# Reordered first loads, merged score matmuls and a split last tile in a fused recurrence and gated-MLP kernel

## Chip, cores, metric

One core of one Trainium2 chip. The metric is the device time of one execution in microseconds (us), as a median over executions; lower is better. The medians quoted are over all runs. A ratio is the mean time of one kernel's fast runs over that of the kernel before in the same rounds on the same chip, so it isn't quite the ratio of the medians that are quoted.

## The reference, cut

```python
# q, k, v, f_logit: (batch 4, heads 8, seq 768, dim 48), float32
f = 1 / (1 + exp(-f_logit))
for t in range(S):
    state = f[:, :, t, :, None] * state + einsum('bhd,bhe->bhde', k[:, :, t], v[:, :, t])
    y[:, :, t] = einsum('bhd,bhde->bhe', q[:, :, t], state)
x = y as (3072 tokens, 384)
out = (relu(x @ w_gate) * (x @ w_val)) @ w_out        # 384 -> 1536 -> 384
```

The kernel cuts the sequence into 6 steps of 128 tokens; a step has 4 chunks, one for each batch. Loads come for two batches at a time ("first pair" and "second pair", written 01 and 23 below). A chunk needs a cumulative sum of log f on TensorE (from f), exponentials on ScalarE, the scaled q and k (called hats), their transpose (qkT), scores, a mask, y, and a state update. The MLP of the step before runs on TensorE in between.

## The kernel before

It is a list scheduler that runs when the kernel is built. Each operation is declared with what it reads and writes and with a planned duration: `occ`, how long it holds its engine, and `lat`, what follows until others may use its result. The scheduler simulates the engines and picks the operation that can start first. The outcome is one fixed order of instructions for each engine. The planned durations are in no instruction; they only decide the order. On the chip each engine goes through its list and waits where an input isn't there yet.

```python
class Plan:
    def schedule(self, banks):
        ...
            for e in self.ENGINES:
                for op in waiting[e]:
                    at = max(free[e], op.ready)
                    ...                                  # a free PSUM bank, if it opens one
                    key = (at, op.prio, op.idx)
                    if pick is None or key < pick[0]:
                        pick = (key, op, slot)
        ...
            op.start, op.end = at, at + op.occ + op.lat
            free[e] = at + op.occ
# --- cut ---
early = ("f0.0.1 f0.1.2 f0.2.3 f0.3.4 k0.0.1 k0.1.2 q0.0.1 q0.1.2 v0.0.1 ...").split()
spread_engines = ['ACT', 'DVE', 'ACT', 'ACT']
pl = Plan({"bc": 1, "tp": 1, "s": 2, "y": 1, "kv": 1, "f": 4, "w": 1})     # banks by kind
pl.settled, pl.margin = 40.0, {"PE": 0.5, "SP": 0.6}
# --- cut: loads are issued by SyncE; so are qkT and x transposes (steps 3 to 5) and stores ---
def cum():
    te.matmul(bc.ap[:, 0:HD], tri[:, :], bn[:, :, 0:D])
    for p in range(NP):
        mm = te.matmul(bc.ap[:, HD + p:HD + p + 1], ..., ones[:, :])
    return mm
chain("cum", "PE", cum, [...], [bc], occ=0.48, lat=PE_L, prio=P, opens=[bc])
# --- cut ---
sA, sB = Bank("s"), Bank("s")
chain("scores", "PE", scores, qk_key, [sA, sB], occ=0.36, lat=PE_L, prio=P + 5, opens=[sA, sB])
```

## Time and profile before

| | before |
|---|---|
| median (range), first 3 runs | 201.19 us (200.59 to 201.33) |
| profiled span | 198.9 us |
| TensorE busy, idle in the span | 192.1 us, 6.8 us |
| TensorE idle in 0-40, 40-105, 105-155 us | 1.62, 0.04, 2.25 us |

The last row comes from the view of busy time by stretch: the width of the stretch minus TensorE's busy time. Its columns are the stretch, its width, then busy us (and instructions) of PE, PEld, DVE, ACT and POOL, the granted clock, the share of busy transfer engines, and GB/s.

```profile
0.00:40.00 40.00, 38.38 (x441) 30.98 (x442) 25.14 (x63) 27.94 (x65) 19.34 (x39) 1.00 1.13 198
40.00:105.00 65.00, 64.96 (x743) 45.48 (x740) 43.82 (x89) 44.06 (x116) 41.62 (x53) 1.00 1.10 209
105.00:155.00 50.00, 47.75 (x398) 25.21 (x399) 26.10 (x41) 28.06 (x57) 16.23 (x20) 1.00 0.81 164
```

The chain of work that ended last (start, us, what) passes through a last transfer at 108.63 and is TensorE alone from 116.13 on:

```profile
99.32 4.14 DMA f_in<-in_f_logit_dram
...
108.63 4.98 DMA q_in<-in_q_dram
...
115.63 0.46 POOL vpad L556
116.13 0.34 PE ps L716 x4
116.48 1.29 PE ps L748 x6
```

SyncE's timeline around the last loads (start, duration with the wait in it, what):

```profile
123.62 1.94 SPq L397 DMA_DIRECT2D f_in<-in_f_logit_dram  x1
125.60 2.73 SPq L785 DMA_DIRECT2D out_dram<-osb  x1
128.78 0.37 SPq L397 DMA_DIRECT2D k_in<-in_k_dram  x1
129.21 2.50 SPq L622 DMA_TRANSPOSE qkT<-hats  x1
```

### The profile page before, as it was taken

To read this page: it belongs to the slowest core of one execution; us is meant where nothing else is said; L and a number is where in the kernel's file an instruction comes from. 1 tells how busy PE (TensorE), PEld (TensorE's weight loads), DVE (VectorE), ACT (ScalarE), POOL (GpSimd) and SP (SyncE) were. 2 spreads that over 40 slices of the span, in tenths; PEclk is the share of its full clock that TensorE was granted. 3 is DMA by queue.
4 is the path that set the end of the run, shared out by engine and by line. 5 is a ranking of instruction groups with operands and counts; after the bars stand their busy time and mean duration, and the time that the engine had idled before them with its cause. 6 is when DMAs were issued, how large, how long until landed. Compare 5 with 4: busy or idle time off the path is not lost.

```text
span 198.9 us, 4530 instructions
## 1 busy us (share of the span) xinstructions
PE 192.1 (97%) x1796; PEld 122.9 (62%) x1796; DVE 107.0 (54%) x208; ACT 115.1 (58%) x263; POOL 77.2 (39%) x111
## 2 busy tenths in 40 slices
PE   7999999999999999999997989999999999999994
PEld 5887588866888787745553535555545555544552
DVE  7258865574399787647737443636265233443300
ACT  2786767906888677867649466386425433344311
POOL 5189303733859668693573174504500000000000
PEclk9999999999999999999999999999999999999999
DMA  4999999999979999999798899988942200111112
GB/s 118 232 225 198 201 214 187 209 222 243 254 173 227 193 240 177 198 212 207 158 213 167 174 185 202 215 171 187 190 112 59 63 31 9 40 40 43 40 71 87
DMA packets 118180, 31.74 MB, mean 160 GB/s; under 512 B 111248, under 2 KB 118160, under 8 KB 118160
## 3 DMA queue, kind: packets, MB, share of 16 engines
q1 hardware_dynamic: 114176, 27.93, 70.3%
q0 software_dynamic: 3984, 3.54, 11.2%
q8 instruction: 14, 0.23, 0.5%
q14 instruction: 6, 0.05, 0.1%
HBM read 25.95 MB, written 4.72 MB: 154 GB/s over the span
## 4 chain that ended last, share of the span: by engine, by line
PE 78%; DMA 10%; SPq 5%; ACT 3%; POOL 2%; issue 1%
PE ps L748 43%; PE ps L770 22%; SPq L397 4%; DMA wv<-in_moe_w_val_dram 4%; PE ps L636 3%; DMA q_in<-in_q_dram 3%; DMA f_in<-in_f_logit_dram 2%; DMA k_in<-in_k_dram 2%; PE ps L613 2%; PE ps L675 2%; PE ps L716 2%; PE ps L671 2%; PE ps L580 1%; ACT relu L755 1%; POOL hats L603 1%; PE ps L582 1%
## 5 line engine op out<-in xcount | busy, mean ns | idle before, releaser
L759 DVE TENSOR_TENSOR gT<-relu,ps 128x256 bf16<-128x256 bf16 (+1 forms) x96 | 52.1, 551 | 59.1 <-PE ps L748 41.4
L748 PE MATMUL ps<-xT,wv 128*128 128x256 bf16 (+1 forms) x288 | 62.5, 326 | 0.5 <-DMA wv<-in_moe_w_val_dram 0.5
L748 PE MATMUL ps<-xT,wg 128*128 128x256 bf16 (+1 forms) x288 | 62.5, 326 | 0.1
L755 ACT ACTIVATE relu<-ps 128x256 bf16<-128x256 f32 (+1 forms) x96 | 46.0, 490 | 27.6 <-PE ps L748 27.3
L770 PE MATMUL ps<-wo,gT 128*128 128x384 bf16 x288 | 52.2, 326 | 0.0
L770 PEld LDWEIGHTS ps<-wo,gT 128*128 128x128 bf16 x288 | 26.6, 97 | 16.8
L748 PEld LDWEIGHTS ps<-xT,wv 128*128 128x128 bf16 x288 | 26.1, 97 | 16.6 <-DMA wv<-in_moe_w_val_dram 0.6
L642 DVE TENSOR_TENSOR ptm<-ps,tri 128x512 bf16<-128x512 f32 x48 | 31.0, 684 | 9.8 <-PE ps L636 9.6
L748 PEld LDWEIGHTS ps<-xT,wg 128*128 128x128 bf16 x288 | 26.6, 98 | 15.2 <-DMA xT<-xn 0.8
L782 ACT ACTIVATE osb<-ps 128x384 f32<-128x384 f32 x24 | 11.7, 491 | 31.7 <-PE ps L770 31.7
L600 POOL TENSOR_TENSOR hats<-k_in,expo 128x384 bf16<-128x384 f32 x20 | 19.9, 997 | 17.6 <-ACT expo L589 17.6
L603 POOL TENSOR_TENSOR hats<-q_in,expo 128x384 bf16<-128x384 f32 x20 | 19.8, 998 | 11.2 <-DMA q_in<-in_q_dram 11.2
L732 POOL TENSOR_TENSOR st<-ssum,dec 128x384 bf16<-128x384 f32 x16 | 13.2, 829 | 14.6 <-DVE ssum L730 14.6
L453 PE MATMUL ps<-zeros 128*128 128x256 bf16 x96 | 14.3, 307 | 1.1 <-DVE zeros L357 1.1
L689 ACT ACTIVATE xn<-ps 128x384 bf16<-128x384 f32 x20 | 9.8, 490 | 6.0 <-PE ps L675 6.0
L556 POOL CAST vpad<-v_in 128x384 bf16<-128x384 f32 x24 | 12.1, 518 | 2.3 <-DMA v_in<-in_v_dram 2.2
L589 ACT ACTIVATE expo<-ps 128x384 f32<-128x384 f32 x20 | 9.8, 491 | 4.0 <-PE ps L582 3.8
L453 PEld LDWEIGHTS ps<-zeros 128*128 128x128 bf16 x96 | 10.1, 110 | 3.2 <-DVE zeros L357 1.1
L570 ACT ACTIVATE f_in<-f_in 128x768 f32<-128x768 f32 x10 | 8.4, 838 | 4.4 <-DMA f_in<-in_f_logit_dram 4.4
L730 DVE TENSOR_TENSOR ssum<-ps,st 128x384 f32<-128x384 f32 x16 | 8.8, 551 | 2.7 <-PE ps L716 2.6
L636 PE MATMUL ps<-qkT 48*128 48x128 bf16 x192 | 9.5, 219 | 0.6 <-DMA qkT<-hats 0.6
L591 ACT ACTIVATE expo<-ps 128x384 f32<-128x384 f32 x20 | 9.9, 495 | 0.0
(71 smaller groups left out, 153.5 us busy)
## 6 DMA issues: line engine op xcount, KB each, us to landing
out_dram<-osb SPq DMA_DIRECT2D x24, 192.0 KB, 2.2
f_in<-in_f_logit_dram SPq DMA_DIRECT2D x10, 384.0 KB, 5.8
k_in<-in_k_dram SPq DMA_DIRECT2D x10, 384.0 KB, 5.2
q_in<-in_q_dram SPq DMA_DIRECT2D x10, 384.0 KB, 5.4
v_in<-in_v_dram SPq DMA_DIRECT2D x10, 384.0 KB, 5.4
wg<-in_moe_w_gate_dram POOLq DMA_DIRECT2D x3, 384.0 KB, 7.2
wv<-in_moe_w_val_dram POOLq DMA_DIRECT2D x3, 384.0 KB, 7.4
wo<-in_moe_w_out_dram POOLq DMA_DIRECT2D x3, 384.0 KB, 7.3
```

The lines of the kernel that those rows point to most:

```text
L453: op = add("PE", lambda: te.matmul(cold.ap[:, 0:256], zeros[:, 0:128], zeros[:, :]), ["zeros"], [cold], occ=0.22 if i < 17 else 0.11, lat= ...
L556: add("POOL", lambda: gp.tensor_copy(vout, vin[:, b, :, :].rearrange("p (n j) d -> p n j d", j=2)), [f"v{li}_{b}", f"vpad{vi}"], [f"v_{vi} ...
L600: add("POOL", lambda: gp.tensor_tensor(hk, kin[:, b, :, :], ex[:, 1, :].rearrange("p (h d) -> p h d", h=H), ALU.mult), [f"k{li}_{b}", f"ex ...
L603: add("POOL", lambda: gp.tensor_tensor(hq, qin[:, b, :, :], ex[:, 0, :].rearrange("p (h d) -> p h d", h=H), ALU.mult), [f"q{li}_{b}", f"ex ...
L636: mm = te.matmul(s.ap[:, p * C:(p + 1) * C], qkT[qi][lo:lo + D, 1, p, :], qkT[qi][lo:lo + D, 0, p, :])
L642: add("DVE", lambda j=j, s=s: ve.tensor_tensor(ptm[mi][:, j, :, :], s.ap[:, :].rearrange("p (n t) -> p n t", n=NP), mask, ALU.mult), [s, " ...
L732: add("POOL", lambda: gp.tensor_tensor(t4(s_new), t4(tmp), rate, ALU.mult), [key] + dk, [f"S{b}_{c % 2}"], prio=P + 8, **pool_t(HD))
L748: mm = te.matmul(bank.ap[:, 0:n], wt[:, kt, j * 128:(j + 1) * 128], xT[xi][:, kt, n0:n1], start=(kt == 0), stop=(kt == NK - 1))
L755: add("ACT", lambda: sc.activation(relu[ri][:, 0:n], gate.ap[:, 0:n], AF.Relu), [gate], [f"relu{ri}"], prio=P, **act_t(n))
L759: add("DVE", lambda: ve.tensor_tensor(gT[gi][:, j, n0:n1], relu[ri][:, 0:n], val.ap[:, 0:n], ALU.mult), [val, f"relu{ri}"], [f"gT{gi}_{j}_ ...
L770: mm = te.matmul(o.ap[:, 0:DM], gT[gi][:, j, b * C:(b + 1) * C], wo[:, j, :], start=(j == 0), stop=(j == NJ - 1))
L782: add("ACT", lambda o=o, oi=oi: sc.activation(osb[oi][:, :], o.ap[:, 0:DM], AF.Copy), [o], [f"osb{oi}"], prio=P, **act_t(DM))
```

## The change

Its intent: k and q of the first pair are loaded ahead of the second pair's f, so that the first scores come earlier; the first spread copies (transposed q and k out of PSUM) start on VectorE; the scores of two chunks stand in one run in steps 4 and 5, so that TensorE goes over to their 48-row form half as often; the last 128 rows of the output are computed as 256 and 128 columns, so that the last copy and store are short. With them three planned durations change: cumulative sum 0.48 to 0.29, scores 0.36 to 0.42 for one chunk and 0.64 for two, and the latency of the zeroing in front of the first matmuls 0.2 to 0.9.

```diff
-    early = ("f0.0.1 f0.1.2 f0.2.3 f0.3.4 k0.0.1 k0.1.2 q0.0.1 q0.1.2 v0.0.1 v0.1.2 ...
+    early = ("f0.0.1 f0.1.2 k0.0.1 k0.1.2 q0.0.1 q0.1.2 f0.2.3 f0.3.4 v0.0.1 v0.1.2 ...
-    spread_engines = ['ACT', 'DVE', 'ACT', 'ACT']
+    spread_engines = ['DVE', 'ACT', 'DVE', 'ACT']
+    TAIL = [0, 256, 384]
+    PAIR = [1, 1, 1, 1, 2, 2]
-    pl = Plan({..., "s": 2, ...})
+    pl = Plan({..., "s": 4, ...})
-    zero("DVE", ve, zeros[:], "zeros", 128, -20)
+    zero("DVE", ve, zeros[:], "zeros", 128, -20, 0.9)          # planned latency
-            chain("cum", "PE", cum, [...], [bc], occ=0.48, ...)
+            chain("cum", "PE", cum, [...], [bc], occ=0.29, ...)
-        chain("scores", "PE", scores, qk_key, [sA, sB], occ=0.36, ...)
+        yield P, qk_key, scores, [sA, sB]
+    def attend(c, bs):
+        works = [attention(c, b) for b in bs]
+        heads = [next(x) for x in works]
+        def scores():
+            for h in heads:
+                mm = h[2]()
+            return mm
+        chain("scores", "PE", scores, [x for h in heads for x in h[1]], sbanks,
+              occ=0.2 + 0.22 * len(heads), ...)
# --- cut: the output projection of the last chunk loops over the column parts of TAIL,
#     each with its own bank, copy and store ---
-        for b in range(B):
-            attention(c, b)
+        n = PAIR[c]
+        for b in range(0, B, n):
+            attend(c, range(b, b + n))
```

More of the change, by code (lines that the diff above doesn't have):

```diff
@@ L240, in bass_hgrn2_outer__then__ffn_reglu_kernel @@
     wsteps = 3
-    early = ("f0.0.1 f0.1.2 f0.2.3 f0.3.4 k0.0.1 k0.1.2 q0.0.1 q0.1.2 v0.0.1 v0.1.2 k0.2.3 k0.3.4 "
+    early = ("f0.0.1 f0.1.2 k0.0.1 k0.1.2 q0.0.1 q0.1.2 f0.2.3 f0.3.4 v0.0.1 v0.1.2 k0.2.3 k0.3.4 "
              "q0.2.3 q0.3.4 v0.2.3 v0.3.4 wg0 wv0 wg1 wv1 wg2 wv2 f1.0.2 k1.0.2 q1.0.2 v1.0.2 wo0 wo1 "
@@ L315, in bass_hgrn2_outer__then__ffn_reglu_kernel @@
     banks = [nc.alloc_psum_tensor(f"ps{i}", [128, 512], F32) for i in range(8)]
-    pl = Plan({"bc": 1, "tp": 1, "s": 2, "y": 1, "kv": 1, "f": 4, "w": 1})
+    pl = Plan({"bc": 1, "tp": 1, "s": 4, "y": 1, "kv": 1, "f": 4, "w": 1})
     pl.settled, pl.margin = 40.0, {"PE": 0.5, "SP": 0.6}
@@ L354, in bass_hgrn2_outer__then__ffn_reglu_kernel, with zero @@
     add("POOL", lambda: gp.memset(ones[:], 1.0), [], ["ones"], occ=0.1, prio=-8)
-    def zero(eng, e, t, name, cols, prio):
-        add(eng, lambda: e.memzero(t), [], [name], occ=0.15 + cols / 2000.0, prio=prio)
-    zero("DVE", ve, zeros[:], "zeros", 128, -20)
+    def zero(eng, e, t, name, cols, prio, lat=0.2):
+        add(eng, lambda: e.memzero(t), [], [name], occ=0.15 + cols / 2000.0, lat=lat, prio=prio)
+    zero("DVE", ve, zeros[:], "zeros", 128, -20, 0.9)
     for i in range(NB):
@@ L584, in cum @@
                 return mm
-            chain("cum", "PE", cum, ["tri", "ones", f"bneg{bi}", f"bn{bi}_{bj}"], [bc], occ=0.48, lat=PE_L,
+            chain("cum", "PE", cum, ["tri", "ones", f"bneg{bi}", f"bn{bi}_{bj}"], [bc], occ=0.29, lat=PE_L,
                 prio=P, opens=[bc])
@@ L638, in scores @@
             return mm
-        chain("scores", "PE", scores, qk_key, [sA, sB], occ=0.36, lat=PE_L, prio=P + 5, opens=[sA, sB])
+        yield P, qk_key, scores, [sA, sB]
         mask = tri[:].unsqueeze(1).to_broadcast([128, NP, C])
@@ L733, in attention @@
                     [key] + dk, [f"S{b}_{c % 2}"], prio=P + 8, **pool_t(HD))
+    def attend(c, bs):
[5 more added lines that the diff above has]
+            return mm
+        sbanks = [x for h in heads for x in h[3]]
+        chain("scores", "PE", scores, [x for h in heads for x in h[1]], sbanks, occ=0.2 + 0.22 * len(heads), lat=PE_L,
+              prio=heads[0][0] + 5, opens=sbanks)
+        for x in works:
+            for _ in x:
+                pass
     def ffn_hidden(c, b0, b1, j):
@@ L764, in ffn_out, with proj_out @@
         gi = g % NG
-        outs = [Bank("f") for b in bs]
-        def proj_out(o, b, s):
+        cuts = TAIL if (g, bs[-1]) == (NC - 1, B - 1) else [0, DM]
+        parts = [(b, n0, n1, Bank("f")) for b in bs for n0, n1 in zip(cuts, cuts[1:])]
+        def proj_out(o, b, s, n0, n1):
             def run():
                 for j in range(s * OJ, (s + 1) * OJ):
-                    mm = te.matmul(o.ap[:, 0:DM], gT[gi][:, j, b * C:(b + 1) * C], wo[:, j, :],
+                    mm = te.matmul(o.ap[:, 0:n1 - n0], gT[gi][:, j, b * C:(b + 1) * C], wo[:, j, n0:n1],
                                    start=(j == 0), stop=(j == NJ - 1))
@@ L773, in proj_out, with rows @@
             return run
-        for s in range(NJ // OJ):
+        def rows(b, n0, n1, o, s):
             js = range(s * OJ, (s + 1) * OJ)
-            for o, b in zip(outs, bs):
-                P = (g + 1) * B * 10 + 5 + NJ * 3 + b * 3
-                chain("ffn", "PE", proj_out(o, b, s), [f"gT{gi}_{j}_{b}" for j in js] + sorted({f"wo{j // WJ}" for j in js}),
-                      [o], occ=pe_t(*[DM] * OJ), lat=PE_L, prio=P + 1000, opens=[o] if s == 0 else [])
-        for o, b in zip(outs, bs):
+            P = (g + 1) * B * 10 + 5 + NJ * 3 + b * 3
+            chain("ffn", "PE", proj_out(o, b, s, n0, n1), [f"gT{gi}_{j}_{b}" for j in js] + sorted({f"wo{j // WJ}" for j in js}),
+                  [o], occ=pe_t(*[n1 - n0] * OJ), lat=PE_L, prio=P + 1000, opens=[o] if s == 0 else [])
+        if len(cuts) > 2:
+            for part in parts:
+                for s in range(NJ // OJ):
+                    rows(*part, s)
+        else:
+            for s in range(NJ // OJ):
+                for part in parts:
+                    rows(*part, s)
+        for b, n0, n1, o in parts:
             oi, P = (g * B + b) % NO, (g + 1) * B * 10 + 5 + NJ * 3 + b * 3
-            add("ACT", lambda o=o, oi=oi: sc.activation(osb[oi][:, :], o.ap[:, 0:DM], AF.Copy), [o], [f"osb{oi}"],
-                prio=P, **act_t(DM))
-            dst = bass.AP(tensor=out.tensor, offset=(b * S + g * C) * DM, ap=[[DM, C], [1, DM]])
-            op = add("SP", lambda dst=dst, oi=oi: sy.dma_start(dst, osb[oi][:, :]), [f"osb{oi}"], [f"out{g}_{b}"],
+            add("ACT", lambda o=o, oi=oi, n0=n0, n1=n1: sc.activation(osb[oi][:, n0:n1], o.ap[:, 0:n1 - n0], AF.Copy), [o], [f"osb{oi}_{x}" for x in TAIL[:-1] if n0 <= x < n1],
+                prio=P, **act_t(n1 - n0))
+            dst = bass.AP(tensor=out.tensor, offset=(b * S + g * C) * DM + n0, ap=[[DM, C], [1, n1 - n0]])
+            op = add("SP", lambda dst=dst, oi=oi, n0=n0, n1=n1: sy.dma_start(dst, osb[oi][:, n0:n1]), [f"osb{oi}_{x}" for x in TAIL[:-1] if n0 <= x < n1], [f"out{g}_{b}_{n0}"],
                      occ=0.2, lat=0.9, prio=P)
-            dma(op, f"osb{oi}", 0.45)
+            dma(op, f"osb{oi}_{n0}", 0.45 * (n1 - n0) / DM)
     OJ = 4
```

## The prediction

> **What bounds the kernel now.** I read the page first (busy shares, the 40 slices), then the chain of work that ended last in order of time, then the waits of TensorE by stretch, then the timeline around the places that the change touches. The page:
>
> ```profile
> PE 192.1 (97%) x1796; PEld 122.9 (62%) x1796; DVE 107.0 (54%) x208; ACT 115.1 (58%) x263; POOL 77.2 (39%) x111
> PE   7999999999999999999997989999999999999994
> DMA  4999999999979999999798899988942200111112
> ```
>
> TensorE is busy nearly throughout, and the transfer engines are full for the first 24 slices (to about 119 us), after which they are nearly idle. TensorE's busy time at the start isn't work, though: 96 of its matmuls multiply zeros (14.3 us). So there are four stretches: a start in which real work waits for data (to about 22 us), a long stretch without a gap on TensorE (22 to 105), a stretch with gaps while the loads are still running (105 to 117), and pure TensorE work (117 to 196) with a tail of one copy and one store. The chain shows the start:
>
> ```profile
> 10.02 4.04 DMA k_in<-in_k_dram
> 14.15 0.95 POOL hats L506
> 15.10 7.03 DMA wv<-in_moe_w_val_dram
> 22.18 0.50 PE ps L748 x3
> 22.68 0.33 PE ps L636 x8
> ```
>
> The hidden layer's second weight (wv, first third) is issued by GpSimd at 15.10, behind a GpSimd product that waits for the second pair's k, and lands at 22.1. From 22.18 the chain is TensorE alone. The first weight (wg) is issued on the same queue at 12.84, behind a cast that waits for v, and took 7.2 us, so it landed at 20.04, while xT of the first pair was ready at 20.03:
>
> ```profile
> 10.70 1.81 DVE L506 TENSOR_TENSOR hats<-q_in,expo 128x384 bf16<-128x384 f32 x2 [4.34 <-DMA q_in<-in_q_dram]
> 12.38 0.51 POOL L556 CAST vpad<-v_in 128x384 bf16<-128x384 f32 x1 [0.29 <-DMA v_in<-in_v_dram]
> 12.84 0.93 POOL L417 DMA_DIRECT2D wg<-in_moe_w_gate_dram  x1
> 20.18 0.24 PEld L748 LDWEIGHTS ps<-xT,wg 128*128 128x128 bf16 x3
> ```
>
> The waits of TensorE between 100 and 118 us, the only real ones after the start (2.18 us unrounded):
>
> ```profile
> PE ps L716 <- POOL vpad L556: 0.9, 1, 0.9
> PE ps L580 <- ACT bneg L573: 0.6, 1, 0.6
> PE ps L636 <- DMA qkT<-hats: 0.6, 1, 0.6
> ```
>
> Behind each stands a transfer: f of step 4 (second pair, issued at 99.32), the transpose of hats, and q and v of step 4 (issued only at 108.63 and 109.26). Last, the timeline around one group of scores, and the tail:
>
> ```profile
> 86.11 0.81 PE L748 MATMUL ps<-xT,wg 128*128 128x512 bf16 x3
> 86.85 0.23 PEld L636 LDWEIGHTS ps<-qkT 48*128 48x128 bf16 x8 [0.42 <-issue]
> 87.18 0.82 PE L748 MATMUL ps<-xT,wv 128*128 128x512 bf16 x3
> ...
> 188.06 7.96 PE L770 MATMUL ps<-wo,gT 128*128 128x384 bf16 x48
> ...
> 196.06 0.49 ACT L782 ACTIVATE osb<-ps 128x384 f32<-128x384 f32 x1 [1.46 <-PE ps L770]
> ```
>
> **What the Trainium skill says.** "TensorEngine Tiling (Array Packing)", Tiling Modes, Key Properties: changing the tiling mode drains TensorE. Scores use 48 of 128 rows, and the trace agrees in kind: 11 times the weight loads of the scores sat idle with nothing to wait for, 3.9 us in total, though most of that lies under matmuls. "TensorE: Matmul & The Clock Gate", Back-to-back issue gap: a matmul of N columns takes N/2.4 + 2.5 ns, but a stream of weight loads with 128-column matmuls about 81 ns each. For 384 columns the trace agrees with the formula (48 matmuls in 7.81 us, 163 ns); for 128 columns the transposes here take 0.45 us for 8, 56 ns, so I use 56 and keep 81 as a risk. "DMA: Bandwidth & Descriptors", Anatomy of one DMA: about 2 us of a transfer are fixed, and only the rest grows with its bytes. The stores here (192 KB) land in 2.2 us (median), which agrees.
>
> **Part 1, the start.** Two loads of f (second pair) move behind k and q of the first pair. An issue takes 0.65 to 0.68 us of the SP queue, so k and q of the first pair start 1.35 us earlier. The second q load was issued at 5.65 and landed at about 10.6; it should land at about 9.2. Also the first cumulative sum came at 8.20 only because 43 zero matmuls stood before it (its input was ready at 6.92); now 37 stand there, and it starts at about 7.5. With copies of 0.67 us on DVE and ACT I get first scores at about 13.4 instead of 15.10 and xT of the first pair at about 17.7 instead of 20.03.
>
> But this gain meets the weights. v of the first pair is issued in the same slot (6.33), so the cast at 12.38 and wg at 12.84 stay; k of the second pair keeps its slot (8.50), so the product at 14.15 and wv at 15.10 stay. wg lands at 20.0, wv at 22.1, as before. What is left of the gain is what TensorE does while it waits for wv: the fourth batch's scores and back transpose are done before 22.1, not after. Between 22.18 and 25.22 the old kernel ran 4 groups of the hidden layer, one scores, two states and two intra products; the new one lacks the scores (0.33) and has fewer changes of mode (some 0.2): TensorE gains about 0.5 us by 25 us. Of this only about 0.3 survives the first cumulative sum of step 1: it stands behind as many hidden matmuls as before (111), ran at 35.64, and its input from ACT was ready at 34.50 + 0.84 = 35.34, tied to a load that is gated by the weights' landing. **Start: 0.3 us.**
>
> **Part 2, scores of two chunks in a run.** The three hidden matmuls at 86.11 need 0.65 us, so scores could start at 86.76; they start at 86.85: 0.09 us for going over. With 8 groups in steps 4 and 5 becoming 4, four such changes go, 4 x 0.09 = **0.36 us**. Nothing is added in instructions; masks and hats are the same. The four banks that two scores hold take DVE four masks of some 0.6 us, 2.6 us in a row, against one hidden pair each 1.3 us; a short TensorE wait for a bank is possible there.
>
> **Part 3, the order of transfers (a consequence).** The built order shows that on the SP queue q of step 4's second pair now goes out before the four transposes of x and hats, right after k (at about 101 instead of 108.63), while its v stays behind them (about 109). On TensorE one hidden group of 0.65 us moves ahead of the cumulative sum that waited 0.64; hidden work of step 3 now starts before step 4's scores. Worked through: that wait shrinks to about 0.3; x of step 3 lands at about 108.3 (the old kernel began that work at 109.74, but with 0.75 us of scores already done); five hidden groups (3.24), 12 output matmuls (1.95) and scores (0.75) lead to 114.25, where the state product waits for v, 109.3 + 5.4 landing + 0.5 cast = 115.3, against 116.13. So TensorE is ahead by about 0.75 us there, which contains the 0.3 of the start: **0.45 us** of its own. After that I find no wait: step 5's loads come earlier than before.
>
> **Part 4, the last rows.** 12 matmuls of 384 columns become 12 of 256 (109 ns) and 12 of 128 (56 ns): 1.31 + 0.67 = 1.98 against 1.95. The last copy has 128 columns: 512 columns take ACT 0.60 and 384 take 0.49, so 0.11 per 128, estimate 0.27, a gain of 0.22. The last store is 64 KB instead of 192 and shares nothing with the first part, which leaves 0.5 us earlier: of the 2.35 us from the copy's end to the span's end I take 0.25 off. **Tail: 0.45 us**, nothing else beside it.
>
> **Sum:** 0.3 + 0.36 + 0.45 + 0.45 = 1.56 us, so 201.19 - 1.6 = **199.6 us**.
>
> **The rivals.** (a) The start's gain arrives whole: xT 2.3 us earlier. For it: nothing on TensorE, DVE or ACT stands against it. Against it: both weights and step 1's load are tied to GpSimd's order and to full transfer engines, and neither moves. It would make 198 us. (b) The loads alone set the time up to 117 us: the same bytes come through engines that are full to then, so parts 1 and 3 give nothing and only 2 and 4 remain, 200.4 us. For it: the DMA row. Against it: one wait in the old kernel came from q waiting behind transposes, not from bytes. (c) A new wait: scores of two chunks need both transposes landed and four free banks, and a static order can't step round a late one; each such wait was 0.4 to 0.9 us in the old kernel. With two of them the gain is gone, 201 us. (d) The last matmuls run at 81 ns: 0.3 us less gain.
>
> **Range and chances.** Runs of the old kernel lie within 0.4%, so the spread is mine, not the clock's. (b) and (c) give 200.4 to 201, (a) 198; I take 198.5 to 200.8. Over 2% means 4.0 us: more than all four parts together with (a). Faster 0.05, within 2% 0.93, slower 0.02.
>
> **What would show it right or wrong.** Right: first scores near 13.4, first hidden matmuls still near 20.1 and wv still landing near 22.1; cumulative sum of step 1 near 35.4, with a small wait; scores in four groups of 16 in steps 4 and 5; one wait of TensorE at about 115 us for the cast of v; the last copy near 0.27 us and the end some 2.1 us after it. Wrong: weights issued earlier than 12.84 and 15.10 (then rival a); waits over 1.5 us in total between 100 and 125 us (b or c); a TensorE wait on DVE right behind the 16 scores (c).

## More of the kernel before

`chain` keeps operations of one kind in their order, so a TensorE order is fully told by how the kinds interleave.

## The result

| | before | after |
|---|---|---|
| median (range), 6 runs each | 200.62 us (200.32 to 201.33) | 203.53 us (202.94 to 204.73) |
| ratio, 95% interval | | 1.0147 (1.0106 to 1.0188) |
| profiled span | 198.9 us | 202.5 us |
| TensorE busy, idle in the span | 192.1, 6.8 us | 191.1, 11.4 us |

Within 2%, but slower by 2.9 us, where 1.6 us of gain was predicted, and above the predicted 198.5 to 200.8 us. The page of the changed kernel (busy time; then PE and DMA in 40 slices of 5.1 us, in tenths):

```profile
PE 191.1 (94%) x1797; PEld 123.4 (61%) x1797; DVE 108.5 (54%) x210; ACT 114.8 (57%) x262; POOL 77.6 (38%) x111
PE   7999999789999999999997999977999999999995
DMA  5999998999999999999987999887962111111113
```

TensorE has new dents: slices 8 and 9 (35 to 46 us) and slices 27 and 28 (132 to 142 us). By stretch:

```profile
0.00:40.00 40.00, 37.47 (x423) 30.12 (x423) 27.58 (x66) 26.85 (x63) 17.99 (x37) 1.00 1.08 191
40.00:105.00 65.00, 62.93 (x733) 44.74 (x734) 42.30 (x85) 43.42 (x113) 41.91 (x53) 1.00 1.08 204
105.00:155.00 50.00, 45.50 (x383) 24.43 (x382) 24.92 (x40) 26.99 (x55) 17.74 (x22) 1.00 0.85 169
```

So idle time went from 1.62 to 2.53, from 0.04 to 2.07, and from 2.25 to 4.50 us: 5.2 us more, of which 0.6 comes back in the tail. With 1.0 us less busy time (0.7 of it zero matmuls, 85 against 96 of them) that is the 3.6 us between the two spans. What TensorE waited for (us in total, times, longest), first between 25 and 60 us, then between 100 and 140 us:

```profile
PE ps L615 <- POOL hats L605: 1.5, 1, 1.5
PE ps L789 <- DMA wo<-in_moe_w_out_dram: 1.2, 1, 1.2
...
PE ps L638 <- DMA qkT<-hats: 1.7, 2, 1.4
PE ps L582 <- ACT bneg L575: 1.3, 1, 1.3
PE ps L766 <- DMA xT<-xn: 1.2, 1, 1.2
```

The early group hangs on one load: q of step 1 landed at 38.6 us instead of 35.6, and the third part of w_out stood behind its consumer on GpSimd. The late group is on steps 4 and 5: hidden work waits for x (xT), a cumulative sum for log f (bneg), scores for qkT. The chain of work now runs from load of f to load of f, and comes back to TensorE only at 138.25 (before: 116.13):

```profile
101.86 4.44 DMA f_in<-in_f_logit_dram
...
113.61 5.51 DMA f_in<-in_f_logit_dram
...
124.48 6.43 DMA f_in<-in_f_logit_dram
...
132.78 2.07 SPq L624
134.85 0.05 issue
134.90 3.25 DMA qkT<-hats
138.16 0.09 issue
138.25 0.62 PE ps L638 x16
```

SyncE's timeline shows what stands between the loads:

```profile
116.83 4.95 SPq L624 DMA_TRANSPOSE qkT<-hats  x2
121.82 0.58 SPq L812 DMA_DIRECT2D out_dram<-osb  x1
...
124.48 1.68 SPq L399 DMA_DIRECT2D f_in<-in_f_logit_dram  x1
126.20 5.07 SPq L707 DMA_TRANSPOSE xT<-xn  x2
131.32 0.58 SPq L812 DMA_DIRECT2D out_dram<-osb  x1
132.35 0.37 SPq L399 DMA_DIRECT2D k_in<-in_k_dram  x1
132.78 3.44 SPq L624 DMA_TRANSPOSE qkT<-hats  x2
```

The Trainium skill, "DMA: Bandwidth & Descriptors", Anatomy of one DMA, says that a transfer's semaphore wait happens on the issuing sequencer, before dispatch. The trace agrees where an input is late: in the kernel before, two transposes of x held SyncE for 4.56 us from 150.38, until 1.2 us after the second one's input was ready (153.74). The two that held SyncE for 5.07 us from 126.20 are another case, as their inputs were there (the copies xn on ScalarE, the second done at 122.86):

```profile
122.35 0.51 ACT L691 ACTIVATE xn<-ps 128x384 bf16<-128x384 f32 x1
...
126.58 1.96 POOL L605 TENSOR_TENSOR hats<-q_in,expo 128x384 bf16<-128x384 f32 x2 [1.66 <-DMA q_in<-in_q_dram]
```

What kept them isn't shown. They stood right behind a load of f; a pair behind a store took 2.50 us (107.71), and with halved loads this pair took 3.40 us (e17 below). Two things stood behind them. The last k load went out at 132.35 instead of 128.78, while its f went out 0.9 us later than before. And the transposes for the next scores, whose hats were done at 128.54 (the second line), went out only at 132.78; in the kernel before the hats were done at 127.67 and the first of the two transposes went out at 129.21. From there comes the wait of 1.37 us at 138.25. On TensorE the same stretch looks so; before, then after:

```profile
132.88 0.33 PE L580 MATMUL ps<-bneg,tri 128*128 128x384 bf16 x1
```

```profile
132.94 0.34 PE L582 MATMUL ps<-bneg,tri 128*128 128x384 bf16 x1 [1.29 <-ACT bneg L575]
138.25 0.62 PE L638 MATMUL ps<-qkT 48*128 48x128 bf16 x16 [1.37 <-DMA qkT<-hats]
```

The cumulative sum runs at the same time, 133 us, in both kernels, because f lands at 130.1 and 130.9. But in the fixed order of the old kernel 420 hidden-layer matmuls stand before it, in the new one 405: five groups of work that could have filled the wait stand behind it.

The tail went as predicted (the copy is 0.28 us, the span ends 2.0 us after it):

```profile
199.54 0.38 ACT L809 ACTIVATE osb<-ps 128x256 f32<-128x256 f32 x1 [0.82 <-PE ps L789]
200.21 0.28 ACT L809 ACTIVATE osb<-ps 128x128 f32<-128x128 f32 x1 [0.29 <-PE ps L789]
```

### The profile page after: what moved, and what is told of

Its sections match the earlier page's. It is cut to its first block, busy times and chain, and to the rows that moved or that the text cites. A ratio compares the mean times of both kernels' runs of the same rounds, so it can differ in the third digit from the quotient of the medians.

```text
span 202.5 us, 4537 instructions
## 1 busy us (share of the span) xinstructions
PE 191.1 (94%) x1797; PEld 123.4 (61%) x1797; DVE 108.5 (54%) x210; ACT 114.8 (57%) x262; POOL 77.6 (38%) x111
## 4 chain that ended last, share of the span: by engine, by line
PE 61%; DMA 21%; SPq 6%; ACT 5%; POOL 3%; issue 2%; DVE 1%
PE ps L766 29%; PE ps L789 18%; DMA f_in<-in_f_logit_dram 8%; DMA q_in<-in_q_dram 4%; PE ps L455 4%; DMA wv<-in_moe_w_val_dram 4%; DMA wo<-in_moe_w_out_dram 4%; SPq L399 3%; PE ps L638 2%; SPq L624 2%; DMA qkT<-hats 2%; PE ps L615 1%; PE ps L677 1%; ACT f_in L572 1%; PE ps L673 1%
## 5 line engine op out<-in xcount | busy, mean ns | idle before, releaser
L789 PE MATMUL ps<-wo,gT 128*128 128x384 bf16 (+2 forms) x300 | 52.1, 319 | 1.2 <-DMA wo<-in_moe_w_out_dram 1.2
L789 PEld LDWEIGHTS ps<-wo,gT 128*128 128x128 bf16 x300 | 27.6, 98 | 18.6 <-DMA wo<-in_moe_w_out_dram 1.6
L809 ACT ACTIVATE osb<-ps 128x384 f32<-128x384 f32 (+2 forms) x25 | 11.8, 477 | 37.8 <-PE ps L789 37.8
L455 PE MATMUL ps<-zeros 128*128 128x256 bf16 x85 | 13.6, 319 | 1.1 <-DVE zeros L359 1.1
L455 PEld LDWEIGHTS ps<-zeros 128*128 128x128 bf16 x85 | 9.3, 115 | 3.3 <-DVE zeros L359 1.1
L638 PE MATMUL ps<-qkT 48*128 48x128 bf16 x192 | 8.7, 218 | 2.0 <-DMA qkT<-hats 1.7
```

The source lines that it names most:

```text
L455: op = add("PE", lambda: te.matmul(cold.ap[:, 0:256], zeros[:, 0:128], zeros[:, :]), ["zeros"], [cold], occ=0.22 if i < 17 else 0.11, lat= ...
L638: mm = te.matmul(s.ap[:, p * C:(p + 1) * C], qkT[qi][lo:lo + D, 1, p, :], qkT[qi][lo:lo + D, 0, p, :])
L789: mm = te.matmul(o.ap[:, 0:n1 - n0], gT[gi][:, j, b * C:(b + 1) * C], wo[:, j, n0:n1], start=(j == 0), stop=(j == NJ - 1))
L809: add("ACT", lambda o=o, oi=oi, n0=n0, n1=n1: sc.activation(osb[oi][:, n0:n1], o.ap[:, 0:n1 - n0], AF.Copy), [o], [f"osb{oi}_{x}" for x in ...
```

## The experiments

All 18 runs at a glance: medians, ratio to the kernel before with its interval, and TensorE's idle time by stretch from the one profiled run of each. All gave the right result but e17 and e18, which are wrong.

| run | this, before (us) | ratio, 95% interval | idle 0-40 | 40-105 | 105-155 |
|---|---|---|---|---|---|
| (the change) | 203.53, 200.62 | 1.0147 (1.0106 to 1.0188) | 2.53 | 2.07 | 4.50 |
| e1 start alone | 201.98, 200.93 | 1.0057 (1.0017 to 1.0096) | 3.02 | 0.67 | 2.27 |
| e2 tail alone | 200.32, 200.93 | 0.9968 (0.9914 to 1.0022) | 2.61 | 0.84 | 1.92 |
| e3 w_out first | 203.92, 200.93 | 1.0141 (1.0099 to 1.0184) | 2.24 | 1.18 | 4.48 |
| e4 runs undone | 206.05, 200.93 | 1.0245 (1.0204 to 1.0286) | 2.98 | 1.91 | 5.31 |
| e5 old order, all parts | 203.88, 200.73 | 1.0155 (1.0112 to 1.0199) | 2.21 | 0.47 | 4.25 |
| e6 new order, no part | 204.67, 200.73 | 1.0136 (1.0077 to 1.0194) | 1.63 | 0.89 | 4.06 |
| e7 old order of SyncE only | 209.89, 200.73 | 1.0449 (1.0401 to 1.0497) | 2.45 | 0.89 | 8.89 |
| e8 old order of TensorE only | 208.16, 200.73 | 1.0349 (1.0298 to 1.0399) | 3.55 | 0.01 | 6.51 |
| e9 old order, no runs | 201.73, 200.98 | 1.0018 (0.9962 to 1.0075) | 2.90 | 0.37 | 2.86 |
| e10 old order, runs alone | 203.19, 200.98 | 1.0104 (1.0052 to 1.0156) | 1.81 | 1.27 | 3.86 |
| e11 cum duration alone | 201.67, 200.98 | 1.0013 (0.9961 to 1.0064) | 2.18 | 1.83 | 1.55 |
| e12 durations back | 200.40, 200.98 | 0.9962 (0.9914 to 1.0009) | 2.39 | 1.55 | 2.94 |
| e13 cums later | 205.22, 200.98 | 1.0213 (1.0173 to 1.0253) | 2.45 | 1.45 | 5.98 |
| e14 cum duration back | 201.85, 200.98 | 1.0046 (1.0005 to 1.0088) | 2.84 | 1.41 | 3.14 |
| e15 scores duration back | 200.87, 200.98 | 0.9992 (0.9947 to 1.0037) | 1.66 | 2.23 | 1.93 |
| e16 durations back, old start | 204.39, 200.98 | 1.0159 (1.0109 to 1.0210) | 2.30 | 0.36 | 4.10 |
| e17 after, half loads | 199.73, 202.86 | 0.9825 (0.9792 to 0.9858) | 3.82 | 2.32 | 0.00 |
| e18 before, half loads | 198.26, 202.86 | 0.9763 (0.9724 to 0.9801) | 2.73 | 1.03 | 0.00 |

Each idle time is from one run, which can lie off the median by more than 1 us (the change's own profile is of a run of 204.63, e10's of 204.41, e15's of 199.42). The last column sorts the kernels with full loads: up to 3.14 us idle the ratio is at most 1.0057, from 3.86 us it is at least 1.0104. The two columns before it don't: e11, e12 and e15 idle 1.55 to 2.23 us between 40 and 105 us, like the change, and lose nothing.

### First batch: which part costs?

**e1**, the start alone; **e2**, the tail alone. Both keep the old planned durations of sums and scores, and their orders came out close to the old one.

```diff
 e1: before, with
+    early = (... k0.0.1 k0.1.2 q0.0.1 q0.1.2 f0.2.3 f0.3.4 ...); spread_engines = ['DVE', 'ACT', 'DVE', 'ACT']
+    zero("DVE", ve, zeros[:], "zeros", 128, -20, 0.9)
 e2: before, with
+    TAIL = [0, 256, 384]
```

> The start's part alone in the kernel before (order of the first loads, spread copies on DVE first, and the zero tile's planned delay), scores, planned durations and last rows as before. The built order then differs from the kernel before only in the first 25 us; the third output weight keeps its place ahead of step 1's product of k on GpSimd. Theory P (the loss comes from the plan that the other parts changed, on GpSimd, in the transfer queue and in TensorE's static order): TensorE stays 0.3 to 0.7 us ahead of the kernel before from 35 us on, no wait between 38 and 47 us, time 0.2 to 0.7 us under the kernel before. Rival L (the new order of the first loads itself makes step 1's q land late, 8.8 us instead of 5.8 in the two profiles, which holds back the third output weight): q of step 1 lands at about 38.5, TensorE waits some 1.2 us or more near 45 us for the output weight, time 1 to 3 us over the kernel before.

> The last rows in two column parts alone in the kernel before; all else stands as there. Both theories: the tail gains 0.4 to 0.5 us (last copy 0.28 instead of 0.49 us, last store 64 KB). In the two profiles the end of TensorE's last matmul is followed by 2.9 us before and 2.3 us after. Time 0.3 to 0.7 us under the kernel before. If it gains nothing, the store's fixed part is all of the tail.

The start alone is slower by about half a per cent, the tail alone a little faster (its interval holds 1). Neither brings the 1.5%. Why the start costs rather than gains isn't settled. Counted by the MLP matmuls done, TensorE is 0.2 us behind the kernel before at 51 us and 1.0 at 104, of 1.2 at its last matmul; one wait lies between, 0.7 us for v (vpad).

**e3**, the change with the third w_out load moved in front of the product of k that it stood behind on GpSimd:

```diff
     order = pl.schedule([bk for bk in banks])
+    # swap the two neighbours on POOL: [product of k, wo2] -> [wo2, product of k]
+    pool[n], pool[n + 1] = pool[n + 1], pool[n]        # with their planned starts
```

> The changed kernel with one swap on GpSimd: the third output weight's load stands ahead of step 1's first product of k again, as in the kernel before. Theory W (the swap is the cause of the waits of 1.46 and 1.22 us near 40 and 45 us): both waits go, time 2 to 3 us under the changed kernel, that is 0 to 1 us over the kernel before. Rival L (q of step 1 lands late whatever GpSimd's order, and the weight waits for that landing): the weight is issued at q's landing in either order, so the wait of about 1.2 us near 45 stays, and the product of k comes later: time as the changed kernel's or up to 1 us over it.

In its profile TensorE is only 0.7 us behind the kernel before at 51 us (the change: 2.4), yet the time stays at 203.92: at 137 us both are 3.8 us behind, so later waits took back what the early one gave. The theory that the wait for w_out is the cause falls.

**e4**, the change with one chunk to a run of scores again:

```diff
-    PAIR = [1, 1, 1, 1, 2, 2]
+    PAIR = [1, 1, 1, 1, 1, 1]
```

> The changed kernel with scores of one chunk at a time in steps 4 and 5 (part 2 undone), all else as changed; the third output weight stays behind the product of k. The waits near 40 and 45 us stay. Theory M (the scores' runs and the order of transfers that comes with them add some 2 us of waits between 105 and 140 us: 4.5 us of TensorE waits in the changed kernel's profile there, 2.2 in the kernel before): time 1 to 2 us under the changed kernel, waits between 105 and 140 near 2.2 us. Rival N (those waits follow from being late by 2.6 us already and from the loads): time within 0.5 us of the changed kernel, or over it by the 0.36 us that the runs save.

Slower by another per cent, so taking the runs out doesn't bring the time back. It is no clean test of the runs, though: the scheduler planned e4 anew, and its last f load went out at 128.86 instead of 124.48. What was left to test was the order itself.

### Second batch: the order, apart from the parts

For e5 to e10 the scheduler got one more rule: TensorE and SyncE must take their kinds of operation in a given sequence. The sequences were read out of the two plans (f is a group of MLP matmuls, c a sum, s scores, and so on).

```diff
                 for op in waiting[e]:
+                    if not op.filler and e in forced and forced[e][done_on[e]] != kind(op):
+                        continue
 e5: after,  PE and SP in the sequence of before  (PE "... 2k 2f c 2f c 6f s f i 4f i 5f c 2f c 3f s i ...")
 e6: before, PE and SP in the sequence of after   (PE "... k 4f c 2f c 6f 2s 2f k 2f i ... 4f c 2f c 3f 2s ...")
 e7: after,  PE as it is, SP in the sequence of before
 e8: after,  SP as it is, PE in the sequence of before
```

> The changed kernel with nothing taken out of it (early loads, spread copies, runs of scores, last rows in two parts), but the scheduler must issue TensorE's chains and SyncE's transfers in the order that the kernel before has; the four merged scores stand where the second of the two stood. Theory O (the loss is the re-planned static order of TensorE and SyncE): 199.3 to 200.8 us, ratio to before 0.993 to 1.001, TensorE's waits between 105 and 155 us back to about 2.2 us from 4.5. Theory L (the loss is the changed start, which shifts when loads and weights land): stays at 202.5 to 204, ratio over 1.010. Theory T (the parts themselves cost, whatever the order): also over 1.010.

> The converse: the kernel before (its own early loads, its own spread copies, scores one by one, last rows in one part), but TensorE's chains and SyncE's transfers stand in the order of the changed kernel; the scores of two chunks stand next to each other but keep their own waits and instructions. Theory O: 202.5 to 206 us, ratio 1.010 to 1.028 (it lacks the start's and the tail's gain). Theory L and T: 200 to 201.5, ratio under 1.005.

> The changed kernel, with TensorE's order as it is, but SyncE's loads, transposing transfers and stores in the order of the kernel before. If the part of theory O that counts is the order of transfers: 199.5 to 201, ratio under 1.003. If it is TensorE's order: 202.5 to 204.5, ratio over 1.010. In between: both share it.

> The changed kernel, with SyncE's transfers in their changed order, but TensorE's chains in the order of the kernel before. If TensorE's order is what counts: 199.3 to 201, ratio under 1.003. If it is the order of transfers: 202.5 to 204.5, ratio over 1.010.

e6 is the clean one: of the change it has only the order on TensorE and SyncE (and the four banks that neighbouring scores need; the other engines were planned anew to fit), and it loses 1.36% (0.77 to 1.94), nearly the whole loss. Its waits are not quite the same ones: 1.8 us for vpad, 1.1 for xT, 0.8 for bneg, 0.3 for qkT. Its stretch from 105 to 155 us:

```profile
105.00:155.00 50.00, 45.94 (x392) 24.58 (x390) 24.78 (x39) 27.69 (x58) 16.81 (x21) 1.00 0.81 168
```

e7 and e8 are far worse than either (their profiles also show a dip of the granted clock, mean 0.983 and 0.992; so do those of e13 and e16 below, 0.992 and 0.983): the two sequences fit each other, and half of one with half of the other leaves TensorE 6.5 to 8.9 us idle. But e5 contradicts my theory as I had put it: with all parts in it, the old order is no better than the new one. Its profile has a wait that neither kernel has, y waiting for masks (2.1 us), and 1.3 us for qkT. That pointed to the merged scores in a place made for single ones.

### Third batch: parts and order together

```diff
 e9:  after with PAIR = [1, 1, 1, 1, 1, 1], PE and SP in the sequence of before
 e10: before with PAIR = [1, 1, 1, 1, 2, 2] and "s": 4, all else in the sequence of before
 e11: before, chain("cum", ...,
-        occ=0.48
+        occ=0.29
 e12: after,
-        occ=0.29                        # cum
+        occ=0.48
-        occ=0.2 + 0.22 * len(heads)     # scores
+        occ=0.36 * len(heads)
```

> Start and tail of the changed kernel, scores one by one, TensorE and SyncE in the order of the kernel before. After the last batch the theory is in two parts: the re-planned order costs (e6: 1.36% by itself), and in the old order the merged scores cost in its place (e5: TensorE waited 2.1 us for masks and 1.3 us for transposed k and q in steps 4 and 5). Then this kernel loses neither: 200.0 to 201.3 us, ratio 0.996 to 1.004, no wait for a mask over 0.5 us after 105 us. If the start costs by itself (rival): 201.5 to 202.5, ratio 1.004 to 1.010.

> Only the scores of two chunks in a run, in steps 4 and 5; start, tail and the order of all else as in the kernel before. If merged scores in the old order wait for the later chunk's k and q and hold up the masks: 201.8 to 203.3 us, ratio 1.006 to 1.014, with waits of y for a mask of over 1 us between 125 and 155 us. If merging costs nothing (rival: the start alone made e5 slow): 199.8 to 201, ratio under 1.003.

> The kernel before with one number changed in what the scheduler believes: a cumulative sum takes 0.29 us instead of 0.48. No instruction is added or taken away, only their order moves. If the planned durations alone bring the loss: 201.8 to 204.5 us, ratio 1.006 to 1.020, with more than 3.5 us of TensorE waits between 105 and 155 us. If the order is only bad together with the parts: 200 to 201.3, ratio under 1.004.

> The whole change, but the scheduler believes the old durations of cumulative sums and scores; it re-plans freely. If the planned durations make the bad order: 200 to 202 us, ratio 0.996 to 1.006. If any re-planning with the parts gives an order as bad: 202.5 to 205, ratio 1.009 to 1.022.

e9 and e10 settle e5: in the old order start and tail together change nothing (1.0018), and the runs alone cost 1.04%. A run can't start before the later chunk's q and k are transposed, and its four masks come late for the first y. TensorE's waits in e10 from 105 us:

```profile
PE ps L687 <- DVE ptm L658: 2.1, 2, 1.5
PE ps L652 <- DMA qkT<-hats: 1.2, 1, 1.2
PE ps L596 <- ACT bneg L589: 0.4, 1, 0.4
```

e12 has every part of the change and another plan, and it is 1.8% faster than the change: nothing differs but two planned numbers and the order that follows from them. Its waits there:

```profile
PE ps L718 <- POOL vpad L558: 2.0, 1, 2.0
PE ps L638 <- DVE gT L777: 0.5, 1, 0.5
PE ps L582 <- ACT bneg L575: 0.3, 1, 0.3
PE ps L638 <- DMA qkT<-hats: 0.2, 1, 0.2
```

The waits for bneg and qkT (3.0 us in the change) are down to 0.5. e11 shows that the changed duration of a sum is not bad by itself: without the other parts its plan is as good as the old one. Only the combination came out badly.

### Fourth batch: which number, which place?

More runs: e13 to e16. They were run on another chip.

```diff
 e13: after, PE sequence near 133 us
-    ... c i f c f s 4f i 2f i 4f c 2f c 3f s ...
+    ... c i f c f s 4f i 2f i 9f c s 2f c ...
 e14: after with occ=0.48 for cum only
 e15: after with occ=0.36 * len(heads) for scores only
 e16: e12 with the old early order, spread_engines and zeroing latency
```

> The changed kernel to the last transfer and product, but TensorE's last two cumulative sums (step 5, second pair of chunks) stand five groups of matmuls later, where the kernel before has them. If their early place is what costs at 133 us (wait of 1.3 us for f): that wait goes, the time falls by 0.5 to 1.3 us, to 202.2 to 203.2, ratio 1.007 to 1.013. If the time is made up by a later wait (the scores' one at 138 us grows, as f lands when it lands): 203.0 to 204.5, ratio over 1.012.

> The whole change, with the planned duration of a cumulative sum back at 0.48 us and that of scores as changed; re-planned freely. If this number makes the order bad: 200 to 201.8, ratio 0.995 to 1.004. If the scores' does: 202.3 to 204.5, ratio over 1.007.

> The whole change, with the planned duration of scores back (0.36 us for each chunk) and that of a cumulative sum as changed (0.29); re-planned freely. If the cumulative sum's number makes the order bad: 202.3 to 204.5, ratio over 1.007. If the scores' does: 200 to 201.8, ratio under 1.004.

> Runs of scores and last rows in two parts with the old planned durations and the old start (f of both pairs first, spread copies as before). If the start is worth nothing or costs: 199.6 to 200.6, ratio 0.992 to 0.998, as fast as with the start (200.4, ratio 0.996) or faster. If the start is worth its 0.3 us or the re-planning falls badly: 200.5 to 202.5, ratio 0.998 to 1.008.

Both e14 and e15 come out within half a per cent of the kernel before: either number back is enough to get another, better plan. So no single number "makes" the bad order. e16 takes away a part that is worth little and lands at 1.0159, worse than both of my expectations. The dip of the clock in e13 and e16 doesn't explain their loss: runs at clock 1.000 took 205.06 and 205.14 us (e13) and 203.37 us (e16). And in e13, where I moved by hand the two sums that seemed too early, the time went up:

```profile
PE ps L652 <- DMA qkT<-hats: 2.6, 1, 2.6
PE ps L780 <- DMA xT<-xn: 1.4, 1, 1.4
PE ps L596 <- ACT bneg L589: 1.1, 2, 0.9
```

The sums that I moved (step 5, second pair) no longer wait. The scores that now wait 2.6 us are the first pair's and need neither of them: their hats were done at 127.66, but their transposes stood on SyncE behind 4.54 us for two transposes of x and went out at 131.39, and the scores started at 137.09. TensorE only came to them sooner. So my reading that the sums' early place costs falls; the wait was moved, not removed.

### Fifth batch: are the loads what the order is too early against?

```diff
 e17: after, e18: before; in load(), for steps 4 and 5
+        if c > 3:      # only the first batch of the pair: half the bytes, wrong on purpose
+            src = bass.AP(..., ap=[[D, C], [S * D, H], [1, D]]); dst = t[:, b0, :, :]
```

> The changed kernel, but each load of steps 4 and 5 brings only the first of its two batches (half the bytes; the result is wrong on purpose for the other batch), every instruction in its place. If the order is bad because it stands too early against loads that land late: waits of TensorE between 105 and 155 us fall from 4.5 to under 2.5 us and the time by 1.5 to 3 us, to 200.5 to 202, ratio 0.998 to 1.007, and the gap to e18 shrinks to under 1 us. If it is bad by the chains within the core (SyncE's transposing transfers waiting in turn for their input), whatever the loads: 202.8 to 204.5, ratio over 1.010.

> The same halved loads in the kernel before. It has 2.2 us of such waits, so at best 198.8 to 200.5, ratio 0.99 to 1.0. If its own waits are not from loads: 200.5 to 201.3.

Every instruction is in its place, only those loads are half as long (the last f load took 3.9 and 3.7 us from issue to landing instead of 6.4 and 6.5). The stretch, for e17 and then e18:

```profile
105.00:155.00 50.00, 50.00 (x420) 27.23 (x418) 27.24 (x44) 29.68 (x59) 17.68 (x22) 1.00 0.67 122
```

```profile
105.00:155.00 50.00, 50.00 (x413) 26.83 (x412) 26.66 (x42) 28.22 (x57) 17.15 (x22) 1.00 0.62 118
```

TensorE never stops in either kernel, and both fell further than I had expected (0.998 to 1.007 and 0.99 to 1.0). The change's time falls 3.2 points of ratio, that of the kernel before 2.4, and 0.6% remains between them (1.0063 = 0.9825 / 0.9763), where 1.47% was. So by these means somewhat more than half of the loss is waits that exist only because loads of steps 4 and 5 take as long as they do (the scatter of the 11 fast runs leaves 0.2 to 1.1% for what remains, by my working); the rest isn't in this stretch (e17 idles 6.1 us before 105 us, e18 3.8).

### The best version

e12 had the lowest ratio with full loads and the right result: 0.9962 with an interval of 0.9914 to 1.0009. The tail alone (e2, 0.9968) is as good within the noise, with one part instead of four. e12 beats the changed kernel clearly and the kernel before by an amount that five rounds don't fully separate from nothing. Its plan is no design that one could have aimed at: e14 and e15, next to it, are 0.3 to 0.8% slower.

## Why the prediction was wrong, point by point

**Part 1, start.** The mechanism held: first scores came at 14.02 (13.4 predicted), wv landed at 21.9 (22.1), and TensorE was 0.66 us ahead at the first sum of step 1 (0.3). But this isn't a gain at the end: alone it costs 0.57% (e1), and with the tail, in the old order, nothing is left (e9).

**Part 2, runs.** The term was too small in place: in the changed kernel a run of 16 takes 0.64 us from the end of the group ahead to the next (115.27 to 115.91), two single ones in the kernel before 0.43 each (123.49 to 123.92), so 0.22 us saved for each run and about 0.9 for four, against 0.36. But it left out what a run costs elsewhere, that it needs both chunks at once: 1.04% in the old order (e10). Undoing it and planning anew was worse (e4).

**Part 3, order of transfers: the step that failed**, with the words "After that I find no wait: step 5's loads come earlier than before". All eight loads of step 5 went out later than before, by 0.7 to 3.9 us (the last f by 0.9, its k by 3.6). I had followed the built order up to 115 us, seen q of step 4 leave earlier, and taken it that the rest would follow. The path of transfers was wrong before that, too: v of step 4 went out at 112.98 and not at 109.3, work on x of step 3, which I had landing at 108.3, began at 111.36, and the state product that I had put at 115.3 ran at 117.68 (116.13 before). TensorE was 2.7 us behind the kernel before at 104 us already (counted by MLP matmuls), mostly from the waits for hats and w_out. Then two transposes of x held SyncE for 5.07 us behind the last f, with the transposes of k and q behind them, and TensorE idled 2.66 us between 125 and 155 us where the kernel before idled 0.05. The order alone costs 1.36% (e6).

**Part 4, tail.** Right: copy 0.28 us (0.27), end 2.0 us after it (2.1). e2 gives 0.6 us in medians, with an interval that holds the predicted 0.45.

**The rivals.** (c), new waits in a static order, was the right kind. Its size was two waits of 0.4 to 0.9 us, which only took the gain away; measured, TensorE idled 4.6 us more in all. It named one of the waits rightly, scores behind their transposes (1.37 us at 138.25); the other, masks behind a run, holds up y only in e5 and e10. (b), the loads set the time to 117 us, was right in that loads bind the middle, but it assumed that their order could do no harm and that the end of it was near 117; in the changed kernel the chain of work passes through loads to 138 us.

**The range.** The spread I allowed came from the sizes of the parts. The spread that mattered is that of re-planning: the plans that the scheduler made freely (the change, e4, e11, e12, e14, e15, e16) lie between 0.9962 and 1.0245, though what they compute hardly differs. I had named no chance for a time above 200.8 us, and 0.02 for over 2% slower, which one such plan (e4) reaches.

**What stays open.** Which single swap in the order does the damage (e13 was one guess, and wrong), why the start alone costs, what holds SyncE in transposes whose inputs are there, and the 0.6% that halved loads leave. The waits before 105 us are in the sum of the one profile, but e3, e11, e12 and e15 show that they don't decide.

## What to carry to other kernels

Where a build-time scheduler fixes the order, a change to any planned duration is a change to the whole order: compare the built orders to the very end, engine by engine, in particular what stands behind slow transfers on the issuing queue, and measure the plan apart from the parts (old parts in the new order, new parts in the old order). A better estimate of one duration isn't a better plan: a sum really takes 0.27 us (132.88 to 133.15 in the kernel before), nearer to the new 0.29 than to the old 0.48. Merging work for a cheaper mode saves a little on the engine and makes it wait for the later of two inputs, so do it where both are long there.

## What the Trainium skill lacked or had wrong

- "DMA: Bandwidth & Descriptors", Anatomy of one DMA, gives 2.0 us plus bytes over 436 GB/s (fitted on GpSimd's path); my estimate from it for a 384 KB load is 2.9 us. With the transfer engines full, loads of that size that SyncE issued between 100 and 125 us took 4.0 to 6.5 us here, q of step 1 8.8 us in one run and 5.8 in another, and the last f load at half the size 3.7 and 3.9. For a plan, the figure for loads that compete is the one that counts, and the page doesn't give one.
- "TensorE: Matmul & The Clock Gate", Back-to-back issue gap, gives about 81 ns for a sustained stream of 128-column matmuls with weight loads. The last rows here have 12 of 256 and 12 of 128 columns in place of 12 of 384, and the whole group took 7.99 us against 7.96, so 165 ns for the two together; with 109 ns for 256 columns that leaves 56 ns for 128, the isolated figure.
- No page that I read tells how long transposing transfers hold the engine that issues them when they stand behind loads: here 5.07 us for two whose inputs were there, against 2.50 us for two behind a store. Nor does any tell what a fixed order costs: here 1.36% of the whole time for the order alone.
